# First blocks of x in halves on two queues, and ScalarE's first table load behind its transfer issues

## The chip, the cores and the metric

The kernel runs on one core of a Trainium2 chip. The metric is the device time of one execution in microseconds (us); the time before is the median of three runs. A core has a matrix engine (TensorE, PE in the profile, with PEld for its weight loads), VectorE (DVE), ScalarE (ACT), GpSimd (POOL) and SyncE (SP). SP and ACT issue the transfers of this kernel, each on a queue of its own (SPq and ACTq in the profile; q1 and q10 among the queues); 16 DMA engines carry out what both queues hold.

## The reference

The input x (2048 rows of 640, bf16) is normalized by row, and two branches use the result:

```python
x = A_q
xn = _layernorm(x, axis=-1)
return x + _A_ref(xn, A_k, A_v, A_shift_k, A_ssm_k, A_ssm_D) \
         + _B_ref(xn, B_w_gate, B_w_up, B_w_down)
# A: kv = (causal 4-tap convolution of k along the rows, by channel) * v
#    y  = causal convolution of kv with ssm_k over 2048 rows (by FFT) + kv * ssm_D;  returns xn * y
# B: h  = sigmoid(xn @ w_gate) * (xn @ w_up)   (640 -> 1728);  returns h @ w_down
```

## The kernel before, in words

The rows are laid out as 128 partitions of 16 blocks: block b of x is the tile `x[:, b, :]`, 128 rows of 640 values, 160 KB. A quarter t of the gated branch takes four blocks, 512 rows.

The gated branch (g for gate, u for up) goes over 14 groups fc of 128 columns; for each, TensorE multiplies five 128x128 pieces of the weights `w` with the transposed normalized rows `xnT`, ScalarE applies the sigmoid and VectorE multiplies into `hT`. `w` holds the columns of w_gate first and those of w_up behind them, and comes in pieces of 256 columns (320 KB, two groups fc) by `load_w` (L182 to L189): u = 0 is the gate (L184), u = 1 the up part (L187). The other branch does the long convolution by a two-stage transform through DRAM, in five chunks of 128 channels; its steps are interleaved with those of the gated branch in an order written out by hand (`ORDER`, L683).

The start of the program stands ahead of that order and is the place of the change:

- ScalarE's first activation is a dummy sigmoid on a 128x4 tile (`warm`, L130). It brings the load of the table that holds the sigmoid.
- Blocks 0 and 1 of x come in halves of 320 columns, the left on SP and the right on ACT (L515). Blocks 2 and 3 come whole, block 2 on SP and block 3 on ACT (L517). Behind them SP issues the first weights: gate and up for fc 0 and 1 (columns 0 to 256), then gate and up for fc 2 and 3.
- TensorE runs 10 matmuls on zeros (L528) meanwhile. VectorE normalizes a block as it comes: two `bn_stats` of 320 columns (L213), `bn_aggr` (L217), an addition (L241), GpSimd's power (L245), and the scaling into `xn` (L250). TensorE transposes `xn` in five pieces (`pt`, L264) and ScalarE copies the result into `xnT` (L267).
- The first products are made block by block (`quarter`, L276) in a list written by hand, so that TensorE can begin with one block of rows. `g10` is the gate product of group 1 for block 0, and `t2` the transposing of block 2:

```python
FIRST = """
g00 g10 t1 u00 u10 t2 g01 g11 u01 u11 t3 g02 u02 g12 u12 g03 u03 g13 u13
"""
```

Behind this list come whole products of 512 rows (L291), from fc 2 on.

Every transfer counts up one of eight semaphores when it lands, and those are handed out in turn. The ninth transfer uses the semaphore of the first again, and the engine that issues it waits until that first one has landed; so on from there.

Of the kernel before, what the change touches and what calls it, by code (L numbers as in the profile page):

```python
# [11 lines left out]
F32 = mybir.dt.float32  # L12
U16 = mybir.dt.uint16
ACT = mybir.ActivationFunctionType
# [5 lines left out]
P = 128  # L20
# [45 lines left out]
def kernel(  # L66
# [14 lines left out]
    nc = tc.nc  # L81
    xr = A_q.flatten_outer_dims().rearrange("(p b) d -> p b d", b=NB)
# [14 lines left out]
    res = ctx.enter_context(tc.tile_pool(name="res", bufs=1))  # L97
# [7 lines left out]
    mhalf = res.tile([P, 4], F32, name="mhalf")  # L105
# [10 lines left out]
    x = res.tile([P, NB, DM], BF16, name="x")  # L116
# [9 lines left out]
    nc.gpsimd.memset(hT[0:64, 13, :], 0.0)  # L126
    nc.gpsimd.memset(wd[0:64, 13, :], 0.0)
    nc.vector.memset(hT[:, 0, :], 0.0)
    warm = res.tile([P, 4], F32, name="warm")
    nc.scalar.activation(warm[:, :], mhalf[:, :], ACT.Sigmoid)  # L130

    sync = nc.sync
    ctx.enter_context(tc.manual_schedule())
# [376 lines left out]
        nc.vector.tensor_tensor(xs, xs, chunks[c]["yx", m][:, :, :], ALU.add)  # L510


    for b in range(2):
        for i in range(2):
            (sync, nc.scalar)[i].dma_start(x[:, b, 320 * i:320 * i + 320], xr[:, b, 320 * i:320 * i + 320])  # L515
    for i in range(2):
        (sync, nc.scalar)[i].dma_start(x[:, 2 + i, :], xr[:, 2 + i, :])  # L517
    for u in range(2):
        load_w(sync, 0, 256, u)
    for u in range(2):  # L520
# [210 lines left out]
```

## Time and profile before

| | us |
|---|---|
| runs | 234.88, 234.98, 235.36 |
| median | 234.98 |
| profiled execution, its own time | 235.94 |
| span of the profiled execution | 234.2 |
| TensorE busy | 227.0 |
| VectorE busy | 204.1 |
| ScalarE busy | 131.5 |

The span runs from the first to the last instruction; 1.7 us of the profiled execution's time lie outside of it, and its time is 0.96 us above the median of the runs. Times in the rows of the profile count from the start of the span. The granted clock of TensorE is full throughout.

### The profile page before, as it was taken

The numbers are of one execution on the slowest core, as the hardware profiler recorded it, in microseconds if no ns is written. First come the engines' busy times: TensorE is split into PE (matmuls) and PEld (weight loads), VectorE is DVE, ScalarE is ACT, GpSimd is POOL, SyncE is SP. The second block draws the span as 40 slices with busy tenths as digits, with TensorE's granted clock in tenths as the row PEclk, the third lists the DMA queues.
The fourth block names the chain that finished last, engine by engine and source line by source line (L and its number), as shares of the span: only waits on it lengthen the run. The fifth ranks groups of instructions, "written<-read, shape, count | busy, mean of one in ns | idle before, by whom it ended". The sixth has DMA issues, their size and how long they took to land.

```text
span 234.2 us, 5584 instructions
## 1 busy us (share of the span) xinstructions
PE 227.0 (97%) x2270; PEld 112.8 (48%) x2281; DVE 204.1 (87%) x323; ACT 131.5 (56%) x191; POOL 12.7 (5%) x27
## 2 busy tenths in 40 slices
PE   7799999999999999999999999999999999999993
PEld 2664444447444444446444444445563545445582
DVE  5532789999969999999999999999999999999574
ACT  2347832438985877866647666855555776652000
POOL 5201200000020000012001000000000000000000
PEclk9999999999999999999999999999999999999999
DMA  6999999799789987978879998999989769784775
GB/s 176 278 305 235 246 344 203 208 243 304 198 270 293 317 213 211 249 164 243 212 261 266 309 272 214 271 227 258 321 200 247 213 180 255 182 217 145 216 266 148
DMA packets 98143, 56.07 MB, mean 239 GB/s; under 512 B 56326, under 2 KB 92358, under 8 KB 97990
## 3 DMA queue, kind: packets, MB, share of 16 engines
q1 hardware_dynamic: 97542, 55.35, 88.2%
q10 hardware_dynamic: 576, 0.36, 0.5%
q8 instruction: 18, 0.29, 0.5%
q14 instruction: 7, 0.06, 0.1%
HBM read 35.39 MB, written 18.35 MB: 229 GB/s over the span
## 4 chain that ended last, share of the span: by engine, by line
PE 79%; DVE 12%; DMA 4%; issue 2%; SPq 1%; ACT 1%; DVEq 0%
PE pg L291 22%; PE pu L291 22%; PE pd L329 14%; PE psb L500 3%; PE pr L340 3%; PE ps L400 3%; PE ps L398 3%; DMA w<-in_B_w_up_dram 3%; PE ps L432 3%; PE psa L461 2%; DVE tmp L377 2%; PE pg L312 1%; DVE acc L379 1%; DVE yx L505 1%; DMA SMt<-tabSM 1%
## 5 line engine op out<-in xcount | busy, mean ns | idle before, releaser
L291 PEld LDWEIGHTS <-w 128*128 128x128 bf16 x500 | 47.1, 98 | 57.4 <-issue 4.0
L291 PE MATMUL pu<-xnT,w 128*128 128x512 bf16 x250 | 62.2, 379 | 0.0
L291 PE MATMUL pg<-xnT,w 128*128 128x512 bf16 x250 | 62.2, 379 | 0.0
L329 PE MATMUL pd<-wd,hT 128*128 128x512 bf16 x213 | 50.4, 379 | 0.7 <-issue 0.2
L306 DVE TENSOR_TENSOR hT<-sig,pu 128x512 bf16<-128x512 bf16 x52 | 34.6, 679 | 12.8 <-ACT sig L300 6.9
L254 ACT CAST t<-ps 128x1024 bf16<-128x1024 f32 x33 | 32.3, 1013 | 21.9 <-PE ps L400 21.9
L300 ACT ACTIVATE sig<-pg 128x512 bf16<-128x512 f32 x52 | 30.6, 598 | 23.7 <-PE pg L291 20.1
L254 ACT CAST xz<-ps 128x1024 bf16<-128x1024 f32 x30 | 29.5, 1015 | 14.3 <-PE ps L432 14.3
L329 PEld LDWEIGHTS <-hT 128*128 128x128 bf16 x224 | 21.3, 98 | 25.1 <-issue 0.9
L447 DVE TENSOR_TENSOR xz<-xz 128x2048 bf16<-128x2048 bf16 x20 | 24.4, 1218 | 0.3
L377 DVE TENSOR_TENSOR tmp<-kx,sc 128x1024 bf16<-128x1024 bf16 x30 | 20.9, 698 | 0.4
L379 DVE TENSOR_TENSOR acc<-acc,tmp 128x1024 bf16<-128x1024 bf16 x30 | 20.6, 685 | 0.5
L505 DVE TENSOR_TENSOR yx<-psb,xn 128x512 bf16<-128x512 f32 x20 | 13.8, 688 | 2.6 <-PE psb L500 1.8
L400 PE MATMUL ps<-kvh,S1t 128*128 128x512 bf16 x40 | 15.5, 387 | 0.0
L254 ACT CAST ao<-psa 128x1024 bf16<-128x1024 f32 x11 | 10.8, 1014 | 8.3 <-PE psa L461 8.2
L398 PE MATMUL ps<-kvh,S1t 128*128 128x512 bf16 x40 | 15.1, 379 | 0.0
L445 DVE STREAM_SHUFFLE xz<-xz 128x512 f32<-128x512 f32 x20 | 14.5, 725 | 0.0
L340 PE MATMUL pr<-wd,hT 128*128 128x128 bf16 x224 | 13.8, 219 | 0.0
L340 PEld LDWEIGHTS <-hT 128*128 128x128 bf16 x224 | 13.0, 98 | 1.8 <-issue 0.6
L334 DVE TENSOR_TENSOR x<-pd,x 128x512 bf16<-128x512 f32 x16 | 10.7, 684 | 2.1 <-PE pd L329 2.0
L257 DVE CAST xz<-ps 128x1024 bf16<-128x1024 f32 x10 | 12.1, 1215 | 0.4 <-PE ps L432 0.4
L500 PEld LDWEIGHTS <-TBt 128*128 128x128 bf16 x160 | 9.7, 98 | 3.4 <-issue 1.5
(57 smaller groups left out, 183.9 us busy)
## 6 DMA issues: line engine op xcount, KB each, us to landing
d<-t SPq DMA_DIRECT2D x20, 512.0 KB, 5.1
t<-d SPq DMA_DIRECT2D x20, 512.0 KB, 5.5
bi<-d SPq DMA_DIRECT2D x8, 512.0 KB, 5.3
d<-ao SPq DMA_DIRECT2D x6, 512.0 KB, 5.7
kvh<-in_A_v_dram SPq DMA_DIRECT2D x10, 256.0 KB, 5.3
kx<-in_A_k_dram SPq DMA_DIRECT2D x10, 256.0 KB, 4.6
hn<-in_A_ssm_k_dram SPq DMA_DIRECT2D x20, 128.0 KB, 4.6
x<-in_A_q_dram SPq DMA_DIRECT2D x3, 640.0 KB, 5.1
```

The source lines that it names most:

```text
L254: nc.scalar.copy(out=out, in_=in_)
L291: nc.tensor.matmul(pg[:, :], lhsT=w[:, c, u * UP + fc * P:u * UP + (fc + 1) * P], rhs=xnT[:, :, c, :], start=(c == 0), stop=(c == NC - 1))
L300: nc.scalar.activation(sig[fc][:, :], pgs[0, fc][:, :], ACT.Sigmoid)
L306: nc.vector.tensor_tensor(hT[:, fc, :], sig[fc][:, :], pgs[1, fc][:, :], ALU.mult)
L329: nc.tensor.matmul(pds[bb][:, :], lhsT=hT[:, fc, bb * P:(bb + 1) * P], rhs=wd[:, fc, 0:4 * P], start=(fc == 0), stop=(fc == NFC - 1))
L340: nc.tensor.matmul(pds[t, b0][:, bb, :], lhsT=hT[:, fc, bb * P:(bb + 1) * P], rhs=wd[:, fc, 4 * P:DM], start=(fc == 0), stop=(fc == NFC - 1))
L377: nc.vector.tensor_tensor(d["tmp"][:, :, :], kx[:, lo + 3 - m:hi + 3 - m, :], sb(m), ALU.mult)
L379: nc.vector.tensor_tensor(d["acc"][:, :, :], d["acc"][:, :, :], d["tmp"][:, :, :], ALU.add)
L398: nc.tensor.matmul(ps[:, 0, :, :], lhsT=S1[:, h, :], rhs=cin[c]["kvh"][:, 0, 4 * n4:4 * n4 + 4, :], start=True, stop=True)
L400: nc.tensor.matmul(ps[:, 1, :, :], lhsT=S1[:, h, :], rhs=hp[:, 2 * n4:2 * n4 + 2, :, :], start=True, stop=True)
L447: nc.vector.tensor_tensor(z[:, 1:3, :, :], z[:, 0:1, :, :].to_broadcast((P, 2, 8, P)), z[:, 1:3, :, :], ALU.mult)
L500: nc.tensor.matmul(ps[:, i, :], lhsT=TB[:, h, 4 * m + i, :], rhs=bi[:, h, 4 * (m % 2) + i, :], start=(h == 0), stop=(h == 1))
```

## The change

Blocks 2 and 3 of x come in halves like blocks 0 and 1, the left half on SP and the right on ACT. So each of the two queues issues four transfers of 80 KB where it issued two of 80 KB and one of 160 KB. The dummy sigmoid, and the table load that comes with it, stand behind ACT's four issues and not behind its first.

```diff
-    warm = res.tile([P, 4], F32, name="warm")
-    nc.scalar.activation(warm[:, :], mhalf[:, :], ACT.Sigmoid)
...
-    for b in range(2):
+    for b in range(4):
         for i in range(2):
             (sync, nc.scalar)[i].dma_start(x[:, b, 320 * i:320 * i + 320], xr[:, b, 320 * i:320 * i + 320])
-    for i in range(2):
-        (sync, nc.scalar)[i].dma_start(x[:, 2 + i, :], xr[:, 2 + i, :])
+    warm = res.tile([P, 4], F32, name="warm")
+    nc.scalar.activation(warm[:, :], mhalf[:, :], ACT.Sigmoid)
     for u in range(2):
         load_w(sync, 0, 256, u)
```

The changed program has two lines less ahead of this place, so that the issues of x stand at L513 in it, `load_w` at L182 and L185, and the dummy sigmoid at L515. In the built program the semaphores are handed out in turn as before, and the waits stand so:

```
before:  SP  x0a  x1a  x2  g(0:256)  u(0:256)  g(256:512) waits for x0b  u(256:512) waits for x0a ...
after:   SP  x0a  x1a  x2a  x3a  g(0:256) waits for x0b  u(0:256) waits for x0a  g(256:512) waits for x1b ...
```

Here x0a is the left half of block 0 and x0b its right half. The order of all else on the five engines is as it was.

## The prediction

> **What bounds the kernel now.** I read the page first, then the chain of waits over the first 14 us, then the timeline there, and last the DMA's rate in small windows.
>
> ```profile
> span 234.2 us, 5584 instructions
> PE 227.0 (97%) x2270; PEld 112.8 (48%) x2281; DVE 204.1 (87%) x323; ACT 131.5 (56%) x191; POOL 12.7 (5%) x27
> 0.00:6.00 6.00, 4.82 (x16) 1.77 (x17) 3.00 (x10) 1.49 (x2) 3.13 (x13) 1.00 0.64 179
> 6.00:12.00 6.00, 4.54 (x70) 3.76 (x68) 3.36 (x11) 2.37 (x4) 1.56 (x3) 1.00 1.06 278
> 228.00:234.00 6.00, 2.46 (x22) 1.45 (x20) 2.62 (x6) 0.00 (x0) 0.00 (x0) 1.00 0.58 159
> ```
>
> The last three rows are windows of 6 us; the first number behind the comma is TensorE's busy time, the last the GB/s of the DMA. TensorE is idle for 7.2 us of the span: 1.2 in the first window, 1.5 in the second, 3.5 in the last, which leaves under 1 us for the 216 us between. So the kernel is TensorE's stream, and what can be won or lost at the start is the moment from which that stream no longer waits. The chain of waits names it (start, length, what):
>
> ```profile
> 2.12 0.43 SPq L184
> 2.55 0.04 issue
> 2.59 6.63 DMA w<-in_B_w_up_dram
> 9.22 0.05 issue
> 9.27 0.73 PE pu L282 x10
> 13.91 1.09 PE pg L291 x5
> ```
>
> The up weights of columns 0 to 256, issued at 2.59, land at 9.22, and from 9.27 on TensorE runs through. Neither x nor the norm is on the chain: the weights come last. The timeline shows the rest of the start:
>
> ```profile
> 0.72 0.41 ACTq L515 DMA_DIRECT2D x<-in_A_q_dram  x1
> 0.73 0.87 SPq L515 DMA_DIRECT2D x<-in_A_q_dram  x2
> 1.16 1.28 ACT L130 ACT_TABLE_LOAD   x1 [1.16 <-PEq L715]
> 1.23 0.40 ACTq L515 DMA_DIRECT2D x<-in_A_q_dram  x1
> 1.65 0.42 SPq L517 DMA_DIRECT2D x<-in_A_q_dram  x1
> 1.65 0.45 ACTq L517 DMA_DIRECT2D x<-in_A_q_dram  x1
> 2.12 0.43 SPq L184 DMA_DIRECT2D w<-in_B_w_gate_dram  x1
> 2.46 0.20 ACT L130 ACTIVATE warm<-mhalf 128x4 f32<-128x4 f32 x1
> 2.59 0.53 SPq L187 DMA_DIRECT2D w<-in_B_w_up_dram  x1
> 2.99 0.89 DVE L213 BATCH_NORM_STATS2 st<-x 128x6 f32<-128x320 bf16 x2 [1.87 <-DMA x<-in_A_q_dram]
> 3.22 0.94 SPq L184 DMA_DIRECT2D w<-in_B_w_gate_dram  x1
> 5.67 0.15 DVE L241 TENSOR_SCALAR lnq<-mv 128x1 f32<-128x1 f32 x1
> 6.05 0.89 DVE L213 BATCH_NORM_STATS2 st<-x 128x6 f32<-128x320 bf16 x2 [0.23 <-DMA x<-in_A_q_dram]
> 6.18 0.69 ACT L267 COPY xnT<-pt 128x640 bf16<-128x640 bf16 x1 [3.52 <-PE pt L264]
> 8.13 0.73 PE L282 MATMUL pg<-xnT,w 128*128 128x128 bf16 x10 [1.34 <-DMA w<-in_B_w_gate_dram]
> 8.30 0.43 DVE L250 TENSOR_SCALAR xn<-x,mv,lnq 128x640 bf16<-128x640 bf16 x1
> 8.70 0.44 PE L264 MATMUL pt<-ident,xn 128*128 128x128 bf16 x5
> 9.84 0.44 PE L264 MATMUL pt<-ident,xn 128*128 128x128 bf16 x5
> 10.11 0.72 PE L282 MATMUL pg<-xnT,w 128*128 128x128 bf16 x10
> ```
>
> And the rate of the DMA (last column) in the same stretch:
>
> ```profile
> 1.70:2.20 0.50, 0.50 (x3) 0.19 (x2) 0.00 (x0) 0.50 (x1) 0.50 (x2) 1.00 0.34 90
> 2.20:3.00 0.80, 0.80 (x4) 0.29 (x2) 0.01 (x1) 0.45 (x2) 0.80 (x2) 1.00 1.08 321
> 3.00:3.70 0.70, 0.70 (x3) 0.17 (x2) 0.70 (x2) 0.00 (x0) 0.04 (x1) 1.00 0.93 155
> 3.70:4.40 0.70, 0.70 (x3) 0.30 (x2) 0.63 (x4) 0.00 (x0) 0.00 (x0) 1.00 0.75 237
> 4.40:5.10 0.70, 0.70 (x3) 0.15 (x1) 0.70 (x3) 0.00 (x0) 0.57 (x1) 1.00 0.93 296
> 5.10:5.70 0.60, 0.60 (x4) 0.13 (x3) 0.57 (x4) 0.00 (x0) 0.00 (x0) 1.00 1.07 323
> 5.70:8.50 2.80, 1.46 (x15) 0.85 (x15) 2.53 (x9) 0.69 (x1) 1.11 (x2) 1.00 1.14 301
> ```
>
> Rate by length, added up, gives what has been moved: 45 KB by 2.2 us, 302 by 3.0, 576 by 4.4, 977 by 5.7. The four blocks of x are 655 KB, each piece of weights 328. The halves of blocks 0 and 1 (328 KB) flow at 321 GB/s; the whole blocks 2 and 3 fall into the stage from 3.0 to 4.4, at 155 to 237. All of x and both first pieces of weights, 1311 KB, have been moved by 5.7 + 334/301 = 6.81, counted in bytes. Yet the second piece lands at 9.22, 2.4 us later. The bytes ahead of it in the count are those of later pieces: some of the 16 DMA engines have run on to them while the slowest still works at x and at the first weights, and a transfer has landed only when its slowest engine has. That lag is 0.4 us for the first half of block 0 (164 KB for block 0 by 2.57, VectorE starts at 2.99), about 1.4 for block 2 (655 KB by 4.67, VectorE starts at 6.05), 2.4 for the weights. It grows out of the slow stage.
>
> **The change part by part.** *The table load.* ACT's second issue, at 1.23, lies inside the table load (1.16 to 2.44), so the load holds no issue up; it costs ACT at most the 0.05 us by which 1.23 is behind SP's second issue. Behind four issues of some 0.42 us it starts at about 2.5 and the dummy ends at 4.0. Next on ScalarE is the copy at 6.18. Gain and loss: none, with 2.2 us of cover; if that were gone, at most the 1.28 of the load.
>
> *The halves.* Per DMA engine the bytes are the same. What I can't read off is whether blocks 2 and 3 as halves flow like blocks 0 and 1 did (321 GB/s, lag small), or whether the slow stage belongs to that moment and stays. At 321 the 655 KB are through at 2.2 + 610/321 = 4.10, against 4.67.
>
> *The wait on SP.* With eight transfers of x all eight semaphores are taken, so SP's first piece of weights waits for x0b. When that lands can be read: in the kernel before, the third piece of weights has this wait and starts at 3.22, 0.10 behind the end of the issue before it (2.59 + 0.53), where such gaps are otherwise 0.04. So the gate piece goes out at about 3.25 in place of 2.12, and the up piece at 3.7 in place of 2.59; queued behind are all of SP's further transfers, and TensorE waits for these two. From issue to full flow the very first transfer took from 0.73 to 2.2, 1.47 us. So the weights flow fully from 4.73. If x is through at 4.10, the DMA idles for about 0.6 us, which is what the smoother x saves. The two pieces have been moved by 4.73 + 656/301 = 6.91, against 6.81.
>
> So, in bytes, nothing is won, and the sum rests on the lag. At 2.4, as now, the up piece lands at 9.3: +0.1. At 1.4, as for block 2, it lands at 8.3: -0.9. At 0.4 to 0.65, it lands at about 7.5, and then something else is late next: block 2. Its statistics can start when VectorE is free, 5.67 + 0.15 = 5.82, instead of 6.05, so its `xn` starts at 8.07 and ends at 8.50; the transposing of block 2, now at 9.84, could begin at about 8.55, so that 1.28 is the most that TensorE can gain. From the ends, +0.1 and -1.28, I take -0.9, the lag of block 2 being the nearest row for a transfer behind a full queue without the long slow stage.
>
> Here a rule speaks against the change. The halves of blocks 0 and 1, 80 KB each, ran at 321 GB/s and the whole blocks of 160 KB at 155 to 237. The Trainium skill, page "DMA: Bandwidth & Descriptors", section "Bandwidth", says the reverse of sizes: batch transfers, and it lists 138 GB/s at 64 KB and 341 at 1 MB. By that figure, an estimate, 328 KB in halves would take 2.4 us in place of about 1.4, the gain would be gone and some loss be left; that is part of the first rival below, and I give the trace more weight since its transfers overlap.
>
> *Does it reach the end?* TensorE idles under 1 us between 12 and 228 us, so a shift of its stream should be passed on. VectorE is the other candidate, and it still waits in the middle, for ScalarE, whose order follows TensorE:
>
> ```profile
> DVE acc L373 <- ACT sc L162: 1.5, 1, 1.5
> ```
>
> I take nine tenths: -0.8 us on the profiled execution, 235.94 to about 235.1. The median of the runs is 0.96 lower than that execution. If this is the cost of profiling, the median gains the same 0.8. If part of it is a worse lag in that one execution, the runs have less to gain. I take -0.6: **234.4 us**.
>
> **The rivals.** *The slow stage stays, or didn't matter.* If the DMA is slow from 3.0 to 4.4 for a reason of its own (x is only 655 KB, the moment is the same, and no row tells size from time), x is through at 4.67, the weights follow as now, and the up piece lands at 9.3. Also if the runs lack the lag of the profiled execution, there is little to win. For it: the 0.96 us. Against: the halves ahead flowed well. It gives 234.9 to 235.1, in any case within 0.2% (0.47 us, about what a measurement of this kernel can tell from no change).
>
> *The wait on SP comes through.* The gate piece needs this long from issue to landing:
>
> ```profile
> DMA to landing us min/median/max: 6.0/6.0/6.0
> ```
>
> If most of it is the path of the slowest DMA engine and not the queue ahead, 3.25 + 6.0 = 9.25 takes the place of 8.13, the up piece follows at 10.3, and TensorE's stream starts 1.1 us later: 236.1 at most. It decides the sign once the up piece lands after 9.7. For it: SP's issue is 1.1 us later for certain. Against: at 2.12 the queue ahead still held nearly all of x, and 610 KB at 301 to 321 GB/s are 2 us of those 6.0.
>
> *The change does less than it says*: the table load hid nothing, as worked out, so this half of it changes no time under any of the cases.
>
> **How the numbers follow.** The lag shrinks and most of it arrives: 0.46, 233.7 (234.98 - 1.28) to 234.5. Stage or lag unchanged: 0.33, 234.5 to 235.4. The wait comes through: 0.21, 235.5 to 236.1. For 8 in 10 the range goes from 233.7 to 235.9, which leaves out the full price of the last case and larger gains than block 2 allows. The signs split, so the likeliest case alone: 233.7 to 234.5. Faster by over 0.2% 0.46, within 0.33, slower 0.21.
>
> **What would show it.** SP's first issue of weights at about 3.25; the table load at 2.5 with nobody waiting; 300 GB/s or more from 3.0 to 4.1, a dip, then 300 from 4.7; block 2's statistics at 5.8; the first up product at 7.8 to 8.4, the transposing of block 2 at 8.6 to 9.0, and the whole stream behind it earlier by that. I am wrong if the rate from 3.0 to 4.4 stays under 240, if the first up product starts at 9.2 or later, or if it starts a microsecond earlier and the end doesn't move.

## The result and the profile after

The changed kernel takes 235.57 us in the median of 22 runs (234.94 to 237.49), the kernel before 234.81 of 22 runs (234.59 to 235.59). The ratio is 1.0032, with a 95% interval of 1.002 to 1.0044: slower by 0.76 us. The forecast was 234.4 and faster.

The profiled execution of the changed kernel says the opposite at first sight: its span is 233.7 us, its own time 235.49, against 234.2 and 235.94 before. A second profile of the unchanged kernel before (span 233.4, own time 235.21) settles this contradiction. Here is the chain of waits of the changed kernel at the start, and behind it that of the second execution of the kernel before (start, length, what):

```profile
0.73 2.42 DMA x<-in_A_q_dram
3.16 0.39 SPq L182
3.59 5.12 DMA w<-in_B_w_up_dram
8.71 0.05 issue
8.76 0.73 PE pu L280 x10
```

```profile
2.17 0.44 SPq L184
2.65 5.57 DMA w<-in_B_w_up_dram
8.26 0.73 PE pu L282 x10
```

In the changed kernel a new link stands at the head of the chain: SP waits for a block of x to land before it issues the first weights, at 3.16 and not at 2.17. The up product begins at 8.76. Before, it began at 8.26 in this execution; the 9.27 belongs to the first profile, an unlucky execution, whose own time lies above all 22 runs of its kernel (235.94 against at most 235.59). Executions like it do occur: one of 27 further runs of the kernel before took 235.91.

What happens at the start arrives almost in full at the end. The first whole product of 512 rows marks it; these are the page's first line and the timeline's row, of the kernel before (second execution), then of the changed one (second execution):

```profile
span 233.4 us, 5595 instructions
...
12.89 1.24 PE L291 MATMUL pg<-xnT,w 128*128 128x512 bf16 x5
```

```profile
span 234.0 us, 5586 instructions
...
13.53 1.24 PE L289 MATMUL pg<-xnT,w 128*128 128x512 bf16 x5
```

The span less that start is 220.5 in both, and 220.3 to 220.6 in all twelve profiled executions of this study. An execution's own time less that start is 222.2 to 222.4. So the medians can be turned into starts: 234.9 means a first whole product at about 12.6, and 235.6 to 235.8 mean 13.3 to 13.5.

The changed kernel's timeline, for the steps that the prediction named:

```profile
2.62 1.28 ACT L515 ACT_TABLE_LOAD   x1 [2.62 <-issue]
3.92 0.20 ACT L515 ACTIVATE warm<-mhalf 128x4 f32<-128x4 f32 x1
5.69 0.88 DVE L211 BATCH_NORM_STATS2 st<-x 128x6 f32<-128x320 bf16 x2
6.27 0.69 ACT L265 COPY xnT<-pt 128x640 bf16<-128x640 bf16 x1 [2.15 <-PE pt L262]
9.33 0.44 PE L262 MATMUL pt<-ident,xn 128*128 128x128 bf16 x5
```

Block 2's statistics come as soon as VectorE is free, and the table load lies in an idle stretch of ScalarE. Neither is on the chain. The DMA's rate in the windows of the prediction (last column; ahead of it the busy share of the DMA engines), first the changed kernel, then the second execution of the kernel before:

```profile
2.20:3.00 0.80, 0.80 (x4) 0.29 (x2) 0.06 (x1) 0.38 (x1) 0.80 (x2) 1.00 1.09 319
3.00:3.70 0.70, 0.70 (x3) 0.16 (x2) 0.70 (x2) 0.70 (x1) 0.04 (x1) 1.00 1.00 163
3.70:4.40 0.70, 0.70 (x3) 0.30 (x2) 0.63 (x4) 0.41 (x2) 0.00 (x0) 1.00 0.88 229
4.40:5.10 0.70, 0.70 (x3) 0.15 (x1) 0.70 (x3) 0.00 (x0) 0.57 (x1) 1.00 0.83 204
5.10:5.70 0.60, 0.60 (x4) 0.18 (x3) 0.56 (x4) 0.00 (x0) 0.00 (x0) 1.00 0.95 236
5.70:8.50 2.80, 2.11 (x23) 1.41 (x21) 2.74 (x10) 0.69 (x1) 1.12 (x2) 1.00 1.02 286
```

```profile
3.00:3.70 0.70, 0.70 (x3) 0.17 (x2) 0.42 (x2) 0.00 (x0) 0.05 (x1) 1.00 0.77 118
3.70:4.40 0.70, 0.70 (x3) 0.30 (x2) 0.67 (x3) 0.00 (x0) 0.00 (x0) 1.00 0.96 280
4.40:5.10 0.70, 0.70 (x3) 0.15 (x1) 0.67 (x4) 0.00 (x0) 0.35 (x1) 1.00 0.96 282
5.10:5.70 0.60, 0.44 (x2) 0.00 (x0) 0.60 (x2) 0.00 (x0) 0.22 (x1) 1.00 1.13 340
5.70:8.50 2.80, 2.35 (x28) 1.57 (x29) 2.64 (x11) 1.01 (x2) 1.11 (x2) 1.00 1.15 301
```

The slow stage from 3.0 stays with the halves (163, then 229). Behind it, from 4.4 to 5.7, the kernel before runs at 282 to 340 on its first weights, and the changed one at 204 to 236. Added up from 1.7 us as in the prediction, 1311 KB (x and both first pieces) have been moved by 6.78 before and by 7.25 after (by 7.08 in the second execution of the changed kernel).

### The profile page after: what moved, and what is told of

Its sections match the earlier page's. It is cut to its first block, busy times and chain, and to the rows that moved or that the text cites. A ratio compares the mean times of both kernels' runs of the same rounds, so it can differ in the third digit from the quotient of the medians.

```text
span 233.7 us, 5597 instructions
## 1 busy us (share of the span) xinstructions
PE 227.9 (98%) x2281; PEld 112.9 (48%) x2281; DVE 204.0 (87%) x323; ACT 131.3 (56%) x191; POOL 12.7 (5%) x27
## 4 chain that ended last, share of the span: by engine, by line
PE 79%; DVE 12%; DMA 4%; issue 1%; ACT 1%; SPq 0%; DVEq 0%
PE pg L289 22%; PE pu L289 22%; PE pd L327 14%; PE psb L498 3%; PE pr L338 3%; PE ps L398 3%; PE ps L396 3%; PE ps L430 3%; PE psa L459 2%; DMA w<-in_B_w_up_dram 2%; DVE tmp L375 2%; PE pg L310 1%; DVE acc L377 1%; DVE yx L503 1%; DVE x L332 1%
## 5 line engine op out<-in xcount | busy, mean ns | idle before, releaser
L327 PE MATMUL pd<-wd,hT 128*128 128x512 bf16 x224 | 51.5, 379 | 0.0
```

Source lines behind the costliest of these rows:

```text
L327: nc.tensor.matmul(pds[bb][:, :], lhsT=hT[:, fc, bb * P:(bb + 1) * P], rhs=wd[:, fc, 0:4 * P], start=(fc == 0), stop=(fc == NFC - 1))
```

## The experiments

The theory: SP's wait, which comes with the seventh and eighth transfer of x, makes the loss. The rivals: the halves as such (shorter rows, more transfers), the place of the table load, and the unlucky execution as the usual one. All ratios are to the kernel before on the same chip, from 5 to 12 executions of each kernel, with a 95% interval. The two columns of starts are from one profiled execution each.

| kernel | first gate piece issued, us | first up product, us | median, us | ratio |
|---|---|---|---|---|
| before, again | 2.17 | 8.26 | 234.97 | 1.0001 (0.9992 to 1.001) |
| table load moved only | 2.11 | 8.40 | 234.97 | 1.0000 (0.999 to 1.001) |
| halves, six transfers | 2.15 | 7.74 | 235.04 | 1.0002 (0.9993 to 1.001) |
| both parts, six transfers | 2.14 | 8.36 | 234.90 | 1.0000 (0.9992 to 1.0009) |
| one issue more on SP | 2.50 | 8.19 | 235.16 | 1.0012 (1.0004 to 1.0021) |
| halves, table load first | 2.59 | 8.09 | 235.03 | 1.0009 (1.0000 to 1.0019) |
| changed, again | 3.00 | 9.04 | 235.84 | 1.0037 (1.0025 to 1.0049) |
| wait only | 3.24 | 8.98 | 235.86 | 1.0038 (1.0025 to 1.0052) |
| longer wait | 3.74 | 8.91 | 235.77 | 1.0044 (1.003 to 1.0057) |
| blocks 2 and 3 on ACT | 1.65 | 8.81 | 235.92 | 1.0043 (1.0031 to 1.0056) |

**The kernel before, again.** No edit.

> The kernel before, unchanged, for a second profile and as the measure of noise: ratio 1.000 within 0.1%. If the profiled execution of before that the prediction rested on was an unlucky one (its 235.94 us lies above all 22 runs), its up weights of columns 0 to 256 land here well before 9.2 us, at some 8.0 to 8.4, the first up product starts then, and the execution's own time is 235.2 or less. If that execution was usual and the 1.1 us are the cost of profiling, the up product starts at 9.1 to 9.3 again and the time is about 235.9.

Measured: up product at 8.26, own time 235.21. The first profiled execution was the unlucky one. This one's own time is still 0.24 us over the median.

**The wait alone.**

```diff
+    tiny = res.tile([1, 2, P], BF16, name="tiny")
+    for i in range(2):
+        sync.dma_start(tiny[:, i, :], Drow[:, i * P:(i + 1) * P])
     for u in range(2):
         load_w(sync, 0, 256, u)
```

> Blocks 2 and 3 whole and the table load first, as before; SP issues two transfers of 256 bytes (to a tile that nobody reads) ahead of the weights, so that all eight semaphores are taken and the first gate piece waits for the right half of block 0, as in the changed kernel. If the wait on SP makes the loss, the gate piece goes out at 3.2 us and the kernel is as slow as the changed one, ratio 1.002 to 1.004 (235.3 to 235.8). If the halves make it, this one is within 0.1% of before.

Ratio 1.0038: the wait alone, with whole blocks and the table load first, is as slow as the change. The two small transfers also take SP 0.60 us to issue, where the change adds one issue of some 0.4 us; what an issue costs without the wait is tested further below. Its chain of waits, and two windows of the DMA:

```profile
3.24 0.41 SPq L184
3.69 5.24 DMA w<-in_B_w_up_dram
8.94 0.05 issue
8.98 0.73 PE pu L282 x10
```

```profile
4.40:5.10 0.70, 0.53 (x3) 0.04 (x1) 0.70 (x2) 0.00 (x0) 0.57 (x1) 1.00 0.55 142
5.10:5.70 0.60, 0.07 (x2) 0.08 (x3) 0.58 (x3) 0.00 (x0) 0.00 (x0) 1.00 0.97 289
```

The DMA engines are busy for 0.55 of the stretch from 4.4 to 5.1: x is nearly through and the weights aren't there yet. That is where this kernel loses. In the changed kernel the gap is shallower: the share is 0.83 in this stretch in its first execution, and in its second there is no gap here (1.04, shown below). So for the changed kernel the gap explains a part of the loss, and how large a part is not shown.

**The halves without the wait.**

```diff
     for i in range(2):
-        (sync, nc.scalar)[i].dma_start(x[:, 2 + i, :], xr[:, 2 + i, :])
+        (sync, nc.scalar)[i].dma_start(x[:, 2:4, 320 * i:320 * i + 320], xr[:, 2:4, 320 * i:320 * i + 320])
```

> Blocks 2 and 3 come in halves of 320 columns, but both blocks in one transfer on each queue: the same rows of 640 bytes and the same bytes by queue as the changed kernel, six transfers of x as before, no wait ahead of the first weights. If the halves (shorter rows, more packets) make the loss, ratio 1.002 to 1.004. If the wait makes it, within 0.1%, or a gain of up to 0.2% if shorter rows help the DMA.

1.0002: the shorter rows cost nothing and bring nothing (each transfer is still 160 KB here). This execution happened to have its weights early, and its chain of waits goes over VectorE: the transposing of block 2 starts at 8.56, the 8.55 that the prediction gave as the earliest. The slow stage is there too, in a row of its windows:

```profile
3.00:3.70 0.70, 0.70 (x3) 0.16 (x2) 0.61 (x2) 0.00 (x0) 0.04 (x1) 1.00 1.04 179
```

**The table load alone.** The two lines of `warm` stand behind the transfers of x, which are as before.

> Only the dummy sigmoid and its table load stand behind ACT's three issues; all else as before. Expected by every theory of the transfers: within 0.1%. If the place of the table load costs anything, slower by up to 0.3%, with ScalarE's first copy later than 6.3 us or its rows waiting for the load.

1.0000, and the first copy of ScalarE is not delayed.

**Both parts without the wait.** The edits of the last two together.

> Both parts of the change without its wait: blocks 2 and 3 in halves of 320 columns, both blocks in one transfer on each queue (six transfers of x), and the table load behind ACT's issues. If the wait is all of the loss, within 0.1% of before, with the gate piece out at 2.1 us and the first up product at 7.7 to 8.4. If the two parts together cost something that neither did alone, 1.002 or more.

1.0000. With the wait taken out of the change, by six transfers of x in place of eight, nothing is left of its loss, nor any gain.

**The changed kernel, again.** No edit.

> The changed kernel, unchanged, for a second profile and timed beside the others. Ratio 1.002 to 1.004; the gate piece goes out at 3.1 to 3.3 us, the DMA falls under 250 GB/s somewhere from 4.4 to 5.7, and the first up product starts at 8.6 to 9.1 us, later than the 8.26 of the second profile of before.

1.0037; the up product at 9.04. The gate piece went out at 3.00, a little earlier than expected. The expectation of under 250 GB/s somewhere from 4.4 to 5.7 failed: the rate is 288 and 286 there. The 223 ahead of it belong to the slow stage of x, and the rate is low behind it, 260 from 5.7 to 8.5 where the kernel before has 301:

```profile
3.70:4.40 0.70, 0.70 (x4) 0.32 (x3) 0.63 (x4) 0.39 (x2) 0.00 (x0) 1.00 0.84 223
4.40:5.10 0.70, 0.53 (x3) 0.03 (x1) 0.70 (x3) 0.00 (x0) 0.40 (x1) 1.00 1.04 288
5.70:8.50 2.80, 1.69 (x19) 1.09 (x20) 2.73 (x11) 0.69 (x1) 1.11 (x2) 1.00 0.99 260
```

**Halves with the table load first.** The changed kernel with the two lines of `warm` back at their old place. The semaphores are handed out in the order in which the built program plans its issues, so the last free one goes to the gate piece, and the right half of block 3 waits instead.

> The halves as in the changed kernel, but the table load first as before. In this order the last free semaphore goes to the first gate piece, and the transfer that has to wait for block 0 is the right half of block 3, on ACT. If the wait ahead of the weights makes the loss, the gate piece goes out at 2.6 us and the kernel is within 0.1% of before. If two transfers more, or the halves as such, cost, it is 1.002 or more. A late block 3 could cost something too; it is needed some 2 us after block 2.

1.0009: within the 0.1% of the first expectation, but its interval reaches to 0.2%. The gate piece goes out one issue later than before, and that delay and the two transfers more are not told apart here; together they cost 0.2% at most.

**One issue more, no wait for the gate piece.** One transfer of 256 bytes on SP ahead of the weights.

> One transfer of 256 bytes on SP ahead of the weights: the first gate piece goes out one issue later, at 2.5 us, without a wait, and the up piece waits for block 0, to 3.2. If the loss comes from the weights' descriptors reaching the DMA engines after x has run out, this costs little, ratio 1.000 to 1.001, since x keeps the engines busy to 4.5 or later. If each microsecond of SP's delay is passed on to the landing, it costs some 0.4 us at the gate piece and 0.6 at the up piece, 1.002.

1.0012: between the two expectations, and the interval holds both. Two kernels, one with halves and one without, agree: with the gate piece at 2.5 to 2.6 and the up piece at 3.1, the cost is 0.1 to 0.3 us. So by these ratios about a third of the loss comes with weights that go out this much later, and the rest with the longer delay that the wait makes. Neither profiled execution shows the small cost: their up products start at 8.19 and 8.09, no later than the 8.26 of the kernel before.

**A longer wait.** Four transfers of 256 bytes in place of two.

> As wait_only, with four transfers of 256 bytes in place of two; the last two wait for block 0, and the gate piece for block 1. It goes out at 3.8 to 4.1 us. If what SP loses ahead of the weights is passed on in full once x no longer covers it, the first up product starts 0.6 to 0.9 us later than in wait_only, at 9.6 to 9.9, ratio 1.006 to 1.008 (236.4 to 236.8). If the delay in wait_only is only the loss of one slot, or something else than the moment of issue, it stays near 1.004.

The expectation failed: 1.0044, not 1.006 or more. SP's rows show that the delay was larger than expected, since the up piece waited for block 2:

```profile
3.74 0.41 SPq L184 DMA_DIRECT2D w<-in_B_w_gate_dram  x1
5.13 0.39 SPq L187 DMA_DIRECT2D w<-in_B_w_up_dram  x1
```

The DMA is at 52 GB/s from 4.4 to 5.1, and the 1311 KB are moved only by 7.65. But the product follows 1.26 us behind that, where it was 1.78 in the kernel with the shorter wait. So the loss doesn't grow with the delay of the issue, as far as the noise lets one see (the intervals of the two ratios overlap): what the empty queue costs is partly won back, in these two executions, by a smaller lag.

**Blocks 2 and 3 on ACT.** A version meant to beat both.

```diff
-    for i in range(2):
-        (sync, nc.scalar)[i].dma_start(x[:, 2 + i, :], xr[:, 2 + i, :])
+    nc.scalar.dma_start(x[:, 2:4, :], xr[:, 2:4, :])
```

> A version that might beat both: SP issues only the left halves of blocks 0 and 1 and goes on to the weights; ACT takes the right halves and then blocks 2 and 3 in one transfer, so that the gate piece goes out at 1.65 us and shares the DMA with blocks 2 and 3. The weights should land earlier (up piece at 7.5 or before, against 8.2 in the second profile of before); blocks 2 and 3 land later, at 5.8 to 6.5. Ratio 0.998 to 1.001: a gain if the weights still come last, nothing or a loss of 0.1% if block 2 then does.

1.0043, outside the expected range. The gate piece is out at 1.65, but block 2's statistics can start only at 7.08, where its landing was expected at 5.8 to 6.5, and the chain of waits goes over it. Neither do the weights come earlier (up product at 8.81):

```profile
7.08 0.89 DVE L213 BATCH_NORM_STATS2 st<-x 128x6 f32<-128x320 bf16 x2 [1.24 <-DMA x<-in_A_q_dram]
```

```profile
3.00:3.70 0.70, 0.70 (x3) 0.16 (x2) 0.69 (x2) 0.00 (x0) 0.04 (x1) 1.00 0.70 92
3.70:4.40 0.70, 0.70 (x3) 0.30 (x2) 0.63 (x4) 0.00 (x0) 0.00 (x0) 1.00 0.48 121
```

Here the transfers in flight from 3.0 to 4.4 are weights in rows of 512 bytes and two whole blocks, and the stage is at its slowest. No version tried beats the kernel before.

## Why the prediction was wrong

*The baseline was the first step that failed.* The prediction took one profiled execution as the kernel, with a lag of 2.4 us between the bytes moved and the landing of the up weights, and let the change bring it to 1.4. In the second execution of the kernel before the lag, counted here to the start of the product, is 8.26 - 6.78 = 1.5 already, and in the changed kernel 8.76 - 7.25 = 1.5 (in its second execution 9.04 - 7.08 = 2.0). Over the ten executions in which the up product waited for its weights it lies between 1.3 and 2.5. The gain of 0.9 us was the distance from an unlucky execution to a usual one. The reason given for the lag, that it grows out of the slow stage, failed with it: the second execution of the kernel before has the slow stage (118 GB/s from 3.0 to 3.7) and not the long lag. The prediction saw the 0.96 us between that execution and the median, gave it a rival's chance of 0.33 with "little to win", and didn't carry it through: with the usual lag on both sides its own sum has no gain left, and the wait remains. That 235.57 lies within the range of 8 in 10, up to 235.9, is no support: the range held both signs.

*The halves flow no better.* The step "at 321 the 655 KB are through at 4.10" failed: it was 4.76. The slow stage from 3.0 to 4.4 stays with rows of 1280 bytes, of 640, and of 512 mixed with 1280 (155 and 237 GB/s, 163 and 229, 92 and 121). A rate that stays under 240 there is what the prediction itself named as a sign of being wrong. So the shorter rows don't remove it; whether the moment or the traffic makes it was not settled.

*So the idle DMA was not paid for.* The term "6.91 against 6.81" was mis-sized: it is 7.25 against 6.78, 0.5 us and not 0.1 (0.3 by the second execution's 7.08). The weights were to flow fully from 4.73, at 301 GB/s; in the first execution they came at 204 and 236 up to 5.7 and at 286 behind it. The same holds over the executions: the four with the wait ahead of the gate piece have moved the 1311 KB by 7.08 to 7.65, the others by 6.64 to 6.94, but for blocks 2 and 3 on ACT (7.09). The issue of the gate piece, predicted for 3.25, was 3.16, and the up piece's 3.7 was 3.59: the wait itself was read right out of one gap of 0.10 us in SP's rows.

*The rival that came true* is the wait, with 0.21, in its sign and its price: "at most 1.1" held (0.76 us by the runs). Its way did not hold: it took the 6.0 us from the gate piece's issue to its landing as fixed, but in the changed kernel the gate product starts 4.5 and 4.9 us behind the issue, at 7.67 and 7.91 and not at 9.25. And its point of decision, an up product after 9.7, was set from the unlucky execution. Taken from the usual one the sign turns at about 8.3.

*What held:* the table load costs nothing (1.0000), and the start is passed on to the end by about the nine tenths that were taken. The earliest and the latest first whole product of the twelve executions lie 1.25 us apart (12.52 with halves in six transfers, 13.77 with blocks 2 and 3 on ACT), the own times of these two 1.10 us (234.84 and 235.94).

*The rule on sizes.* The halves in six transfers changed the rows and not the size, 160 KB each. Transfers of 80 KB for all four blocks, without the wait ahead of the weights, are in the kernel with the table load first, and its 1.0009 leaves 0.2% at most for them. The Trainium skill, page "DMA: Bandwidth & Descriptors", section "Bandwidth", would have small transfers lose much of the rate; with several in flight no run here shows it. The skill's page "Trainium Kernel Development and Optimization", section "Key Constraints", says that the queues of SP and ACT run on the same DMA engines and that issuing from several only saves the issue time. The two versions with six transfers don't speak against it: with blocks 2 and 3 each on both queues the kernel is no faster (1.0002 and 1.0000).

What stays open: why the landing lags by 1.3 us in one execution and 2.5 in another, and what slows the DMA from 3.0 to 4.4. That some of the 16 engines run ahead of a slowest one, as the prediction has it, is not shown, since no row tells one DMA engine from another. On the slow stage the packets recorded in the traces say a little more: in every one of the twelve executions 8 to 17 single packets take over 0.2 us each from 3.0 to 4.4, where the median packet of data takes 0.03 to 0.06, and they make up 0.14 to 0.40 of the time that the DMA's packets take there. Their cause is not known.

## What to carry to other kernels

Count the transfers in flight against the semaphores: two small transfers more put one issue and a wait for a landing ahead of the first weights, which went out about a microsecond later; that, and not the shorter rows or the table load, cost 0.3%. Before forecasting from a start-up wait in one profile, compare that execution's own time with the runs; if it lies outside them, the wait it shows may be that execution's alone. And the length of a wait on the issuing engine isn't its price: a gate piece later by 0.5 us and an up piece later by 1.4 cost no more than the shorter wait (1.0044 and 1.0038).

## What the runs showed of the hardware

A table load doesn't hold up the transfers issued by the same engine: ACT's second issue at 1.23 lies inside the load from 1.16 to 2.44, and moving the load changed no time (1.0000). The first product on the up weights came 1.3 to 2.5 us after as many bytes as x and both first pieces hold, counted over all 16 DMA engines, had been moved, in the ten executions in which it waited for these weights. And the same program's up weights landed a microsecond apart in two executions (9.22 and 8.2 us).
